# Windowed attention with sinks and a gated MLP block: products of a constant tile put into TensorE's queue before and between the first pairs of heads, and a third load buffer

## The chip, the cores and the metric

The kernel runs on one core of one Trainium2 chip. The metric is the device time of one execution in microseconds (us). A core has five engines with a queue of instructions each, which they work through in order: PE (TensorE, the matrix array; its weight loads are shown apart as PEld), DVE (VectorE), ACT (ScalarE), POOL (GpSimd) and SP (SyncE, which here only issues DMAs).

## What is computed

There are 4 batches, 8 heads, 768 positions and 64 columns per head, all in float32. Attention keeps a window of 128 positions back and the first 4 positions ("sinks"); its output, put together to rows of 512, goes through a gated MLP with a mixing over positions.

```python
def _attn_ref(q, k, v, n_sink, window):          # (4, 8, 768, 64); n_sink 4, window 128
    scores = scale * np.matmul(q, k.transpose(0, 1, 3, 2))
    keep = is_sink | in_window                   # pos < 4, or 0 <= row - pos < 128
    scores = np.where(keep, scores, -1000000000.0)
    ...
    a = a / (np.sum(a, axis=-1, keepdims=True) + 1e-09)
    return np.matmul(a, v)

def _moe_ref(x, w_in, g_ln, w_sg, b_sg, w_out):  # x (4, 768, 512), w_in (512, 1024)
    h = x @ w_in                                 # then gelu (tanh form)
    u, v = (h[..., :d_ff // 2], h[..., d_ff // 2:])
    v_n = (v - mu) / np.sqrt(var + 1e-06) * g_ln
    v_s = np.einsum('ts,bsd->btd', w_sg, v_n) + b_sg[None, :, None]
    return x + (u * v_s) @ w_out
```

## The kernel before, in words

**The unit of work is a pair of heads.** There are 16 pairs, numbered n, four to a batch. A pair has 6 tiles of 128 positions. Its k and q come by two DMAs of 384 KB on SP (`load_qk`, line 80) into float32 buffers `k_sb` and `q_sb` of the pool `loads`, which holds 2 of each. The first pair's come in halves, k on SP and q on ACT's queue (`load_first`, line 95). v comes on POOL's queue, converted to bf16 on the way (`load_v`, line 87), and so do the 4 sink rows of all heads (`vsink`, line 141) and the weights (`load_weights`).

**From load to transposed columns.** `repack` (line 191) has POOL cast k and q to bf16. `keys` and `queries` transpose the six tiles on PE (`to_columns`, line 197: six products with an identity into the PSUM tile `cps`) and ACT copies them out as `kT` and `qT` (line 204). For keys POOL also copies the 4 sink columns to `sk` (line 214). The first pair goes a way of its own, `prepare_first`: for each half of the positions, DVE casts k and q (line 230), PE transposes three tiles of each (line 234), ACT copies k's columns and DVE q's (lines 238 and 240).

**Scores and values.** `score(n, g)` makes four products (line 260) for two of the six tiles and one exponential on ACT (line 264) from PSUM tile `sc`, of which there are two, shared with the sink scores `scs` (line 275, exponential in line 277). `keep_band` multiplies by the band on DVE (line 271). `values(n, i)` multiplies the exponentials with v (lines 305, 308, with the sinks 311) into the PSUM tile `av`, of which there is one; after three tiles DVE takes the reciprocals and scales into `x` (lines 315, 316). `columns` transposes x to `xT` (line 286).

**The order is written out by hand.** Ahead of the loop come the loads of pairs 0 and 1, constants, `prepare_first`, and then `load_qk(2)`, `repack(1)`, `load_v(1)`. In step n of the loop POOL gets `repack(n + 2)`, `load_v(n + 2)` and a part of the weights; PE gets the scores of pair n (groups g = 0, 1, 2), between them the values of pair n - 1, the transposes of keys n + 1 and, in the first batch, of queries n + 1; SP gets `load_qk(n + 3)` after the scores. In step 0 the keys and queries of pair 1 come last, after the sink scores. A load waits until the cast of the pair that had its buffer has read it.

**The MLP** of a batch follows one step after its four pairs: `hidden` makes the products with the input weights (lines 333 and 345, gelu on ACT), and the mixing over positions (line 383) and the output (lines 397 to 409) are queued as fillers among the next batch's scores. A last part of the program, behind a branch, is a slower and safer path that these inputs don't take.

Of the kernel before, what the change touches and what calls it, by code (L numbers as in the profile page):

```python
# [8 lines left out]
F32 = mybir.dt.float32  # L9
BF16 = mybir.dt.bfloat16  # L10
# [7 lines left out]
def kernel(  # L18
# [14 lines left out]
    nc = tc.nc  # L33
# [14 lines left out]
    NH = S // 2  # L48

    consts = ctx.enter_context(tc.tile_pool(name="consts", bufs=1))  # L50
    loads = ctx.enter_context(tc.tile_pool(name="loads", bufs=2))
    work = ctx.enter_context(tc.tile_pool(name="work", bufs=2))
    small = ctx.enter_context(tc.tile_pool(name="small", bufs=4))
    ps_s = ctx.enter_context(tc.tile_pool(name="ps_s", bufs=2, space=PSUM))
    ps_a = ctx.enter_context(tc.tile_pool(name="ps_a", bufs=1, space=PSUM))
# [5 lines left out]
    HT = NT // 2  # L61
# [13 lines left out]
    def load_qk(n):  # L75
        b, hp = divmod(n, HP)
        pair = []
        for src, name in ((k, "k_sb"), (q, "q_sb")):
            dst = loads.tile([128, 2, NT, 64], F32, name=name)
            nc.sync.dma_start(out=dst, in_=src[b, 2 * hp:2 * hp + 2].rearrange(  # L80
                "h (p t) d -> p h t d", t=NT))
            pair.append(dst)
        qk[n] = pair

    def load_v(n):
        b, hp = divmod(n, HP)
        nc.gpsimd.dma_start(  # L87
            out=v_bufs[n % NV][:, :, :, 0:64],
            in_=v[b, 2 * hp:2 * hp + 2].rearrange("h (t p) d -> p h t d", p=128))

    def load_first():
        pair = [loads.tile([128, 2, NT, 64], F32, name=name) for name in ("k_sb", "q_sb")]
        for a in range(2):
            for src, dst, queue in ((k, pair[0], nc.sync), (q, pair[1], nc.scalar)):
                queue.dma_start(
                    out=dst[:, :, HT * a:HT * (a + 1), :],
                    in_=src[0, 0:2, NH * a:NH * (a + 1)].rearrange(
                        "h (p t) d -> p h t d", t=HT))
        qk[0] = pair

    load_first()
    load_qk(1)
    for t in v_bufs[0:2]:
        nc.vector.memset(t[:, :, :, 64:65], 1.0)

# [21 lines left out]
    def copy_masks():  # L127
        nc.vector.tensor_copy(mask0, mask)
        for hl in range(2):
            nc.vector.memset(mask0[0:n_sink, 2 * hl, :], 1.0)  # L130
        for hl in range(2):
            nc.vector.tensor_copy(mask_end[:, 384 * hl:384 * hl + 256], mask[:, 0, :])
            nc.vector.tensor_copy(mask_end[:, 384 * hl + 256:384 * (hl + 1)],
                                  mask[:, 0, 0:128])
# [52 lines left out]
    def repack(n, eng):  # L187
        packed[n] = []
        for src, name in zip(qk.pop(n), ("k_bf", "q_bf")):
            flat = work.tile([128, NT, 128], BF16, name=name)  # L190
            eng.tensor_copy(flat.rearrange("p t (h d) -> p h t d", h=2), src)  # L191
            packed[n].append(flat)

    def to_columns(src, pool, tag):
        ps = pool.tile([128, NT, 128], BF16, name="cps", tag=tag)
        for t in range(NT):
            nc.tensor.transpose(ps[:, t, :], src[:, t, :], iden)  # L197
        return ps

    def copy(eng, dst, src):  # L200
        dst = dst.rearrange("c (p t) -> c p t", t=NT)
        src = src.rearrange("c t p -> c p t")
        if eng is nc.scalar:
            eng.copy(dst, src)  # L204
        else:
            eng.tensor_copy(dst, src)
# [9 lines left out]
    def queries(n, eng, pool, tag):  # L216
        qps = to_columns(packed.pop(n)[1], pool, tag)
        qTs[n] = work.tile([128, S], BF16, name="qT")
        copy(eng, qTs[n], qps)

    def prepare_first():
        flats = [work.tile([128, NT, 128], BF16, name=name) for name in ("k_bf", "q_bf")]
        qTs[0] = work.tile([128, S], BF16, name="qT")
        kT, sk = kT_bufs[0], sk_bufs[0]
        for a in range(2):
            ts = slice(HT * a, HT * (a + 1))
            for src, flat, dst, eng, pool, tag in (
                    (qk[0][0], flats[0], kT, nc.scalar, ps_t, "tp"),
                    (qk[0][1], flats[1], qTs[0], nc.vector, ps_m, "mm")):
                nc.vector.tensor_copy(  # L230
                    flat[:, ts, :].rearrange("p t (h d) -> p h t d", h=2), src[:, :, ts, :])
                ps = pool.tile([128, NT, 128], BF16, name="cps", tag=tag)
                for t in range(HT):
                    nc.tensor.transpose(ps[:, t, :], flat[:, HT * a + t, :], iden)
                to = dst[:, NH * a:NH * (a + 1)].rearrange("c (p t) -> c p t", t=HT)
                frm = ps[:, 0:HT, :].rearrange("c t p -> c p t")
                if eng is nc.scalar:
                    eng.copy(to, frm)
                else:
                    eng.tensor_copy(to, frm)  # L240
            if a == 0:
                for hl in range(2):
                    rows = slice(64 * hl, 64 * hl + 64)
                    nc.gpsimd.tensor_copy(sk[rows, 32 * hl:32 * hl + n_sink],
                                          kT[rows, 0:n_sink])
                score(0, 0)
        qk.pop(0)

    def score(n, g):
        kT, qT = kT_bufs[n % NB], qTs[n]  # L250
        if g == 0:
            exps[n] = work.tile([128, NT * 512 - 256], BF16, name="ex")
        ex = exps[n]
        sc = ps_s.tile([128, 2, 512], F32, name="sc", tag="s")
        w = 0
        for j in (2 * g, 2 * g + 1):
            n_q = min(256, S - 128 * j)
            for hl in range(2):
                rows = slice(64 * hl, 64 * hl + 64)
                nc.tensor.matmul(sc[:, hl, w:w + n_q], kT[rows, 128 * j:128 * (j + 1)],  # L260
                                 qT[rows, 128 * j:128 * j + n_q], start=True, stop=True)
            w += n_q
        part = ex[:, 1024 * g:1024 * g + 2 * w].rearrange("p (h c) -> p h c", h=2)
        nc.scalar.activation(out=part, in_=sc[:, :, 0:w], func=AF.Exp, scale=scale)  # L264

    def keep_band(n, g):
        w = 1024 if g < HT - 1 else 768
        part = exps[n][:, 1024 * g:1024 * g + w]
        m = mask0 if g == 0 else mask
        m = m.rearrange("p a c -> p (a c)") if g < HT - 1 else mask_end  # L270
        nc.vector.tensor_mul(part, part, m)  # L271
# [8 lines left out]
    def by_dma(n):  # L280
        return n >= HP and n % HP < HP - 1
# [135 lines left out]
    def fill(count=1):  # L417
        for _ in range(count):
            if fillers:
                fillers.pop(0)()  # L420
# [142 lines left out]
        V.tensor_copy(mask[:, i, :], mask[:, 0, :])  # L563
    prepare_first()
    copy_masks()
    load_qk(2)
    repack(1, G)
    load_v(1)
    prepare_rest()
# [1 line left out]
    for n in range(NP):  # L571
        if n + 2 < NP:
            repack(n + 2, G)
            load_v(n + 2)
        load_weights(n)
        late = half_valued == n - 1

        def value(i):
            if n > 0 and (i >= HT or not late):
                values(n - 1, i)  # L580

        points = (HT + 1) * ((HP - n) % HP)

        def spread(left):
            if n > HP * (B - 1):
                fill(1 if left > 2 or (left == 1 and n < NP - 1) else 0)
            else:
                fill(-(-len(fillers) // (points + left)))

        for g in range(HT):  # L590
            if n + g > 0:
                score(n, g)
            if g < 2 and not late:
                for i in range(HT * g, HT * (g + 1)):
                    value(i)
            if g == 0 and n > 0 and n + 1 < NP:
                keys(n + 1)
                if n < HP:
                    queries(n + 1, A, ps_m, "mm")
            if g == 0 and late:  # L600
                for i in range(HT, NT):
                    value(i)
            keep_band(n, g)
            if g == 1 and n + 1 < NP and n >= HP:
                queries(n + 1, A, ps_t, "tp")
            spread(HT + 1 - g)
        if n + 3 < NP:
            load_qk(n + 3)
        sinks(n)
        if n == 0:  # L610
            keys(1)
            queries(1, A, ps_m, "mm")
        if n > 0 and not by_dma(n - 1):
            columns(n - 1)
        spread(1)
        if n % HP == 0 and n > 0:
            fill(len(fillers))
            hidden(n // HP - 1, [lambda i=i: values(n, i) for i in range(HT)])
            half_valued = n
# [58 lines left out]
```

## Time and profile before

| | |
|---|---|
| time, median of 3 runs | 180.08 us (179.92 to 180.32) |
| the profiled execution | 180.66 us, of which 178.8 us from the first to the last instruction |
| busy, share of the span | PE 88%, PEld 50%, DVE 82%, ACT 67%, POOL 32% |
| PE products / POOL instructions | 1407 / 98 |
| moved by DMA | 27.24 MB, 152 GB/s on the mean |
| chain that ended last | PE 75%, ACT 12%, issue 4%, DVE 4%, DMA 2% |

All of it is from the page of one profiled execution. A row of slices cuts the span in 40 equal parts of 4.47 us; each digit is the busy share in tenths. A row of the timeline begins with its start and its length in us, then engine, line and operation, the tile written and the tile read, and in brackets how long the engine was idle before it and what ended that. Matmuls overlap and their ends are modelled, so the distance between starts says more than one length. A row of a DMA queue gives packets, MB and the time that its packets took, as a share of the time of 16 engines; q1 is SP's queue, q0 POOL's, q10 ACT's.

### The profile page before, as it was taken

The page shows a single profiled execution, that of the slowest core. Times are in us where ns is not written, and L with a number is a line of the kernel's source. Part 1 is how long each engine was busy: PE and PEld are TensorE (multiplying, and loading weights), DVE is VectorE, ACT ScalarE, POOL GpSimd, SP SyncE. Part 2 cuts the span into 40 slices and gives each one's busy share as a digit, 9 for nine tenths or more (in the row PEclk, how much of TensorE's full clock was granted, in tenths as well). Part 3 has the DMA queues.
Part 4 walks back from the last instruction along what each step waited for, and adds up shares of the span by engine and source line. Part 5 has one row for each costly group of instructions (what it writes and reads, how often), then busy time and mean ns, then how long its engine had stood idle before and what let it go on. Part 6 is the DMA issues. An engine that isn't in the chain of part 4 may idle for free.

```text
span 178.8 us, 3744 instructions
## 1 busy us (share of the span) xinstructions
PE 156.6 (88%) x1407; PEld 88.7 (50%) x1418; DVE 146.0 (82%) x359; ACT 119.4 (67%) x168; POOL 57.5 (32%) x98
## 2 busy tenths in 40 slices
PE   0769779799689999899899999899799999999970
PEld 0447556345556555445456545355465554555430
DVE  5665989599889999698999998699999948858950
ACT  2488999867938668666968668877986856640000
POOL 8459999950042060425006070550010000000000
PEclk9999999999999999999999999999999999999999
DMA  5999999999857739895285969986202241011072
GB/s 158 266 306 265 267 271 273 191 207 218 103 179 48 202 66 209 303 270 39 20 219 33 214 183 192 380 108 44 44 4 44 50 178 59 0 63 60 0 294 66
DMA packets 47974, 27.24 MB, mean 152 GB/s; under 512 B 33680, under 2 KB 44944, under 8 KB 47952
## 3 DMA queue, kind: packets, MB, share of 16 engines
q0 software_dynamic: 27904, 6.31, 37.5%
q1 hardware_dynamic: 19504, 20.26, 37.5%
q10 hardware_dynamic: 544, 0.39, 0.7%
q8 instruction: 12, 0.20, 0.5%
q14 instruction: 10, 0.08, 0.1%
HBM read 24.81 MB, written 6.29 MB: 174 GB/s over the span
## 4 chain that ended last, share of the span: by engine, by line
PE 75%; ACT 12%; issue 4%; DVE 4%; DMA 2%
PE vs L383 17%; PE hu L345 13%; PE o_ps L397 11%; PE hv L333 11%; ACT ex L264 7%; PE sc L260 7%; PE cps L197 5%; PE av L305 4%; ACT kT L204 3%; PE scs L275 2%; PE av L308 2%; DMA k_sb<-in_k_dram 2%; ACT qT L204 2%; PE av L311 1%; DVE ex L271 1%
## 5 line engine op out<-in xcount | busy, mean ns | idle before, releaser
L264 ACT ACTIVATE ex<-sc 128x1024 bf16<-128x1024 f32 (+1 forms) x48 | 45.6, 958 | 16.9 <-PE sc L260 16.7
L383 PE MATMUL vs<-wsgT,vn 128*128 128x384 bf16 x192 | 35.5, 327 | 0.5 <-DVE wsgT L182 0.4
L191 POOL CAST k_bf<-k_sb 128x768 bf16<-128x768 f32 x15 | 12.3, 823 | 42.7 <-DMA k_sb<-in_k_dram 31.8
L397 PE MATMUL o_ps<-w_out_sb,gT 128*128 128x512 bf16 (+1 forms) x93 | 23.8, 370 | 1.2 <-DVE o_sb L401 0.8
L271 DVE TENSOR_TENSOR ex<-ex,mask 128x1024 bf16<-128x1024 bf16 x32 | 23.0, 722 | 1.8 <-ACT ex L264 1.7
L333 PE MATMUL hv<-w_in_sb,xT 128*128 128x512 bf16 x92 | 22.2, 379 | 1.9 <-DVE xT L286 1.7
L383 PEld LDWEIGHTS <-vn 128*128 128x128 bf16 x192 | 17.9, 98 | 12.0 <-issue 1.2
L345 PE MATMUL hu<-xT,w_in_sb 128*128 128x384 bf16 x128 | 23.2, 325 | 0.1
L260 PE MATMUL sc<-qT,kT 64*128 64x256 bf16 x192 | 19.0, 280 | 2.2 <-DVE qT L240 1.3
L386 DVE SCALAR_TENSOR_TENSOR gv<-vs,g_sb,b_bc 128x384 bf16<-128x384 f32 x32 | 19.5, 611 | 1.7 <-PE vs L383 1.7
L348 ACT ACTIVATE uT<-hu 128x384 bf16<-128x384 f32 x32 | 15.7, 490 | 6.5 <-PE hu L345 6.3
L337 DVE BATCH_NORM_STATS2 st<-v_all 128x6 f32<-128x512 f32 x24 | 16.3, 677 | 4.6 <-ACT v_all L335 4.5
L335 ACT ACTIVATE v_all<-hv 128x512 f32<-128x512 f32 x24 | 14.3, 597 | 7.2 <-PE hv L333 6.9
L316 DVE TENSOR_TENSOR x<-av,inverses 128x384 bf16<-128x384 f32 x32 | 17.8, 557 | 1.1
L305 PE MATMUL av<-v_sb,ex 128*128 128x65 bf16 x192 | 18.2, 198 | 0.2 <-DVE x L316 0.2
L305 PEld LDWEIGHTS <-ex 128*128 128x128 bf16 x192 | 14.5, 100 | 7.2 <-issue 2.9
L345 PEld LDWEIGHTS <-w_in_sb 128*128 128x128 bf16 x128 | 12.4, 97 | 10.7 <-issue 2.9
L87 POOL DMA_DIRECT2D v_sb<-in_v_dram x16 | 16.6, 1036 | 0.0
L308 PE MATMUL av<-v_sb,ex 128*128 128x65 bf16 x160 | 16.5, 197 | 0.0
L214 POOL COPY sk<-kT 64x4 bf16<-64x4 bf16 x30 | 6.2, 207 | 28.2 <-ACT kT L204 27.3
L191 POOL CAST q_bf<-q_sb 128x768 bf16<-128x768 f32 x15 | 14.1, 938 | 3.0 <-DMA q_sb<-in_q_dram 2.2
L333 PEld LDWEIGHTS <-xT 128*128 128x128 bf16 x96 | 9.0, 98 | 11.9 <-DVE xT L286 2.6
(83 smaller groups left out, 241.4 us busy)
## 6 DMA issues: line engine op xcount, KB each, us to landing
k_sb<-in_k_dram SPq DMA_DIRECT2D x15, 384.0 KB, 5.5
q_sb<-in_q_dram SPq DMA_DIRECT2D x15, 384.0 KB, 6.1
out_dram<-o_sb SPq DMA_DIRECT2D x17, 256.0 KB, 3.5
v_sb<-in_v_dram POOLq DMA_DIRECT2D x16, 192.0 KB, 6.9
out_dram<-o_act SPq DMA_DIRECT2D x6, 256.0 KB, 2.0
wsg_sb<-in_moe_w_sg_dram POOLq DMA_DIRECT2D x2, 576.0 KB, 10.2
w_in_sb<-in_moe_w_in_dram POOLq DMA_DIRECT2D x4, 256.0 KB, 8.9
w_out_sb<-in_moe_w_out_dram POOLq DMA_DIRECT2D x1, 512.0 KB, 11.8
```

The costliest lines, as they stand in the source:

```text
L191: eng.tensor_copy(flat.rearrange("p t (h d) -> p h t d", h=2), src)
L260: nc.tensor.matmul(sc[:, hl, w:w + n_q], kT[rows, 128 * j:128 * (j + 1)], qT[rows, 128 * j:128 * j + n_q], start=True, stop=True)
L264: nc.scalar.activation(out=part, in_=sc[:, :, 0:w], func=AF.Exp, scale=scale)
L271: nc.vector.tensor_mul(part, part, m)
L305: nc.tensor.matmul(av[:, m, hl, :], probs(i, hl, 0), v_sb[:, hl, i, :], start=(m == 0 and hl == 0), stop=False)
L308: nc.tensor.matmul(av[:, m, hl, :], probs(i - 1, hl, 1), v_sb[:, hl, i - 1, :], start=False, stop=False)
L316: nc.vector.tensor_mul(x_sb[b][:, hp, HT * c:HT * (c + 1), :].rearrange("p i (h d) -> p i h d", h=2), av[:, :, :, 0:64], rcp.to_broadcast( ...
L333: nc.tensor.matmul(h_ps, xT[b][:, c, 128 * j:128 * (j + 1)], w_in_sb[:, c, DF:], start=(c == 0), stop=(c == KD - 1))
L345: nc.tensor.matmul(h_ps[:, 0:NH], w_in_sb[:, c, 128 * f:128 * (f + 1)], xT[b][:, c, NH * n:NH * (n + 1)], start=(c == 0), stop=(c == KD - 1))
L383: nc.tensor.matmul(vs[:, 0:NH], vns[b][:, si, 128 * f:128 * (f + 1)], wsgT[:, si, cols], start=(si == 0), stop=(si == NT - 1))
L386: nc.vector.scalar_tensor_tensor(out=gv, in0=vs[:, 0:NH], scalar=g_sb[:, f:f + 1], in1=b_bc[:, cols], op0=ALU.mult, op1=ALU.add)
L397: nc.tensor.matmul(o_ps, gTs[b][:, c, rows], w_out_sb[:, c, cols], start=(c == 0), stop=(c == KU - 1 and whole))
```

## The change

The pool `loads` gets 3 buffers of each tile, and `load_qk(2)` moves from behind `prepare_first` to right behind `load_qk(1)`. DVE sets a tile of 128 x 128 to ones, and a function `keep_busy(count)` has PE multiply this tile with itself that many times, into a PSUM tile that takes the place of `av` and is never read. It is called with 28 ahead of all other work on PE, with 7 at the end of each of the two halves of `prepare_first` (behind its transposes and copies, ahead of the first scores), with 6 after the last scores of step 0, and with 8 after the queries of pair 1.

```diff
-    loads = ctx.enter_context(tc.tile_pool(name="loads", bufs=2))
+    loads = ctx.enter_context(tc.tile_pool(name="loads", bufs=3))
...
     load_first()
     load_qk(1)
+    load_qk(2)
+    warm = consts.tile([128, 128], BF16, name="warm")
+    nc.vector.memset(warm, 1.0)
+    warm_ps = ps_a.tile([128, HT, 2, 65], F32, name="warm_ps", tag="av")
+
+    def keep_busy(count):
+        for _ in range(count):
+            nc.tensor.matmul(warm_ps[:, 0].rearrange("p h d -> p (h d)")[:, 0:128],
+                             warm, warm, start=True, stop=True)
+
+    keep_busy(28)
     for t in v_bufs[0:2]:
...
                     eng.tensor_copy(to, frm)
+            keep_busy(7)
             if a == 0:
...
     copy_masks()
-    load_qk(2)
     repack(1, G)
...
             if n + g > 0:
                 score(n, g)
+            if n == 0 and g == HT - 1:
+                keep_busy(6)
...
             queries(1, A, ps_m, "mm")
+            keep_busy(8)
```

## The prediction

> **What bounds the kernel now.** I read the page's slices first, then the products by shape before and after 18 us, then the order of time up to 30 us, the windows and the DMA queues.
>
> ```profile
> PE   0769779799689999899899999899799999999970
> ACT  2488999867938668666968668877986856640000
> PEclk9999999999999999999999999999999999999999
> ```
>
> Each slice is 4.47 us. From about 38 us the PE row is full, and the chain of waits is nearly all PE; a gain made earlier is kept if nothing else is late. The clock row shows nothing of a slow start, but the durations do. The groups by shape, first for 0 to 18 us, then for 19 to 33 us (the column after the bar is the mean of one in ns):
>
> ```profile
> L260 PE MATMUL sc<-qT,kT 64*128 64x256 bf16 x20 | 3.0, 400 | 2.2 <-DVE qT L240 1.3 <-ACT qT L204 0.9
> L197 PE MATMUL cps<-iden,k_bf 128*128 128x128 bf16 x12 | 1.7, 313 | 0.0
> L275 PE MATMUL scs<-qT,sk 128*128 128x512 bf16 x2 | 1.2, 596 | 0.8 <-ACT ex L264 0.8
> ...
> L260 PE MATMUL sc<-qT,kT 64*128 64x256 bf16 x26 | 2.8, 274 | 0.0
> L197 PE MATMUL cps<-iden,k_bf 128*128 128x128 bf16 x18 | 1.5, 219 | 0.0
> L275 PE MATMUL scs<-qT,sk 128*128 128x512 bf16 x3 | 1.1, 376 | 2.2 <-ACT ex L264 2.1
> ```
>
> The same shapes are 220 ns faster for 512 columns and 94 ns for 128, so the array runs at half rate at first. The timeline fixes the moment: six transposes from 17.66 still take 0.68, four score products at 18.27 take 0.39 (0.61 before). Twelve transposes in a row from 13.76 are 0.107 apart, those from 18.97 0.056. The windows say what came before: PE was busy 4.55 of 7.50 us in 5.00 to 12.50 without a switch, then 5.61 of 5.70 in 12.50 to 18.20, with the switch at the end.
>
> ACT then is the limit of pairs 2 to 4: 14.13 busy of 14.30 us in 18.20 to 32.50. Timeline rows, start and length:
>
> ```profile
> 4.38 0.50 PE L234 MATMUL cps<-iden,k_bf 128*128 128x128 bf16 x3 [4.38 <-DVE k_bf L230]
> 4.89 0.50 PE L234 MATMUL cps<-iden,q_bf 128*128 128x128 bf16 x3
> 5.43 0.56 DVE L240 COPY qT<-cps 128x384 bf16<-128x384 bf16 x1 [0.59 <-PE cps L234]
> 7.45 0.56 DVE L240 COPY qT<-cps 128x384 bf16<-128x384 bf16 x1 [0.92 <-PE cps L234]
> ...
> 6.69 1.02 ACT L264 ACTIVATE ex<-sc 128x1024 bf16<-128x1024 f32 x1 [1.30 <-PE sc L260]
> 8.70 1.73 ACT L264 ACTIVATE ex<-sc 128x1024 bf16<-128x1024 f32 x2 [0.61 <-PE sc L260]
> 13.23 1.02 ACT L264 ACTIVATE ex<-sc 128x1024 bf16<-128x1024 f32 x1 [0.70 <-PE sc L260]
> 14.72 0.80 ACT L204 COPY kT<-cps 128x768 bf16<-128x768 bf16 x1 [0.47 <-PE cps L197]
> 18.71 1.02 ACT L264 ACTIVATE ex<-sc 128x1024 bf16<-128x1024 f32 x1
> 19.63 0.79 ACT L204 COPY kT<-cps 128x768 bf16<-128x768 bf16 x1
> 23.24 1.02 ACT L264 ACTIVATE ex<-sc 128x1024 bf16<-128x1024 f32 x1
> ```
>
> Before 18 us ACT idles behind PE (the brackets); after it, it doesn't. So what the change can win is how much earlier ACT reaches the first exponential of pair 2, at 18.71.
>
> **The change part by part.**
>
> *28 products first.* They need a memset (0.07, before DVE's first one at 1.01), so PE starts near 1.15 and at 0.107 each ends near 4.15. The first transposes wait for a cast until 4.38: they cost nothing, with 0.2 us of cover. They make PE's work nearly unbroken from 1.15 on. How long that takes to double the rate the trace bounds by at most 5.6 us (12.6 to 18.2): the switch then falls between 4.4, from which on it matters, and 6.8. I take 6.8, the one length that the trace shows to be enough.
>
> The Trainium skill's page "TensorE: Matmul & The Clock Gate" (Part 4: PE-mode transpose) says against this that transposes don't count as busy in the same way. By it the stretch with 12 transposes after 4.38 might not count, and the switch would come only after 12 us: the sum below would be -0.95 less the DMA term. The trace bears it out only in part, since the stretch before 18.2 holds 24 transposes and did switch.
>
> *Seven after each half of the first pair.* They stand behind q's transposes and ahead of the scores, which wait for DVE's copy. At half rate: 4.89 + (3 + 7) x 0.107 = 5.96, and the scores began at 6.04; in the second half 6.88 + 1.07 = 7.95 against 8.06. The cover is 0.1 us even at half rate: nothing. The six (0.34 at full rate) lie under the exponential that the sinks product waits for, the eight (0.45) under ACT's copies of pair 1.
>
> *What full rate from 6.8 changes.* Up to 6.65 nothing moves. The second scores (8.06) wait for ACT's copy of k's second half, 7.61 + 0.47, as before; they take 0.39, not 0.61, so ACT starts their exponential at 8.47 (was 8.70). ACT is then closed: 1.70 to the sinks exponential, 0.64 to the keys and 0.69 to the queries of pair 1, whose copy starts at 11.50 (was 11.73). The scores of pair 1 come 0.86 after that, at 12.36, and take 0.42 with the handover, not 0.64: exponential at 12.78, **-0.45**. From it to ACT's copy of the next keys took 1.49 (13.23 to 14.72), behind values and transposes at half rate; the same step is 0.92 one pair later (18.71 to 19.63): **-0.57**. From there to the next pair's exponential took 3.99 (14.72 to 18.71), and takes 3.61 where ACT is closed (19.63 to 23.24): **-0.38**. Together -1.40: pair 2's exponential at 17.31. With full rate from 4.4 on the first scores too end earlier (6.26, not 6.65), which adds 0.37.
>
> *Third pair's loads early.* They go out on SP directly behind the second pair's, at about 2.8 and 3.3 instead of 6.28 and 6.76, and every later pair finds a buffer one pair sooner. What it gives: POOL's cast of pair 2 waits less. What it costs: 768 KB stand ahead of v's loads.
>
> ```profile
> 11.94 0.82 POOL L191 CAST k_bf<-k_sb 128x768 bf16<-128x768 f32 x1 [1.91 <-DMA k_sb<-in_k_dram]
> ...
> q1 hardware_dynamic: 158, 0.24, 85.5%
> ...
> q1 hardware_dynamic: 753, 1.09, 105.2%
> ```
>
> The cast can begin at 10.0. ACT wants these keys at 13.7, and even before they were cast by 12.76 and the queries by 13.8: worth 0 to 0.1. The two queue rows are of 8 to 10 and of 10 to 13 us: full speed is 363 GB/s, thus 2.2 us for a pair, and 8 to 10 us moved only 0.29 MB in all (0.05 on POOL's queue), so 1.3 us of that was unused and is filled now. The need for v, moved up with the chain: v of pair 0 (requested at 2.28, 8.2 to landing) goes from 10.5 to at most 12.7, wanted at 12.6 (first value product, 13.13 before). The last sink rows (11.3) go to 13.5, wanted at 12.9: 0.6 late, ahead of pair 2's transposes on PE, whose copy would then start at 14.1, not 13.7. v of pair 1 (8.96 + 7.5 = 16.5) goes by 2.2 - 1.3 to 17.4, wanted at 17.2 (18.59 before), 17.6 if the sink rows were late. Pair 3's has 0.2 to spare. The last quarter of the input weights (27.04 + 9.3 = 36.3, used at 38.01) has no more bytes ahead of it than before, and POOL asks for it earlier: nothing. So between 0 (requests on POOL's queue not held up) and 0.6; the landings are worked out at their latest, so I take **+0.3**.
>
> *Later.* SP waits once less per load; POOL's long waits for loads after 50 us are a pair ahead of need. PE, ACT and DVE do the same work after pair 0: nothing.
>
> Sum: -0.45 - 0.57 - 0.38 + 0.30 = -1.1. The profiled execution took 180.66 with 178.8 of span (1.86 outside it); it would take 179.56. The 0.58 that it lies above the median is not touched, so from the median of 180.08: **179.0**.
>
> **The rivals.**
>
> *Slower: v starved.* If the DMA engines served SP's queue until it is empty, v of pair 0 would wait for pairs 2, 3 and 4: SP's requests of 6.28 and 7.58, which were for pairs 2 and 3, are now for 3 and 4 and keep the queue full to 7.1 + 3 x 2.2 = 13.7, not 7.1. v lands 6.6 - 1.3 = 5.3 later, at 15.8. Values of pair 0 stand on PE ahead of pair 2's transposes and start 2.7 late; the 0.95 after it stays: +1.7, or 181.8. It decides from a landing later than 14.1. For it: from 10 to 13 us POOL's queue moved nothing, although v of pair 1 had been issued by 10.02. Against it: order of arrival explains that too, and from 17 to 18 us POOL's queue had 182.1% and SP's 25.7% with a load of SP's requested at 16.84.
>
> The skill's page "DMA: Bandwidth & Descriptors" (Queues, rings and completion order) states a round robin between queues. By it v would share from its issue on, land before its need, and the +0.3 would fall away: -1.4. The row of 10 to 13 us speaks against it.
>
> *Same: no earlier switch,* since a product of ones doesn't count or the gaps at 4.2 and 4.8 reset it. The products are covered at half rate too, so nothing moves but loads: 180.1.
>
> *Same or little: given back.* v's landings 1.3 worse (the unused time from 8 to 10 us isn't there to fill): v of pair 1 at 18.7, 0.1 later than used before; what is left is 0 to 0.4: 179.9.
>
> *More: earlier switch and no late v.* -1.40 - 0.37: 178.3.
>
> **How the numbers follow.** Forecast (-0.4 to -1.5): 0.56. Earlier switch: 0.12. No switch 0.05 and given back 0.10. Starved: 0.17. A measurement of this kernel tells 0.2%, 0.36 us, from no change. Faster 0.68, same 0.15, slower 0.17. The range leaves out only the starved case: from 178.2 (the earlier switch, less 0.1 of spread between runs) to 180.3 (given back, plus the 0.2 to 0.4 by which the runs spread).
>
> **What would show it.** Score products of about 280 ns from 8 us on instead of 400; pair 1's first exponential near 12.8 and pair 2's near 17.6; ACT closed from 13 to 31; the first hidden product near 31.8 (was 32.94); POOL's cast of pair 2 near 10. I am wrong if the rate is half past 9 us, if values of pairs 0 or 1 wait for a DMA by over 0.6 us, or if the first hidden product moves by 1 and the end doesn't.

## The result, and the profile after

Before: 180.2 us (179.92 to 180.67, 4 executions); after: **186.14 us** (184.76 to 187.50, 4). The ratio is 1.0303 [1.0255, 1.035]: the change makes the kernel slower by 3%, where 179.0 was forecast and the range ended at 180.3. The profiled execution took 186.01, of which 184.2 of span, 5.4 more than before. A ratio given here leaves out the few executions that ran clearly longer than the rest of the same kernel; medians are over all.

The slices of the page (4.6 us each):

```profile
PE   7842967879969999989979999899799999999970
ACT  2661889987793776767796687967987667650000
PEclk9997599999999999999999999999999999999998
```

The PE row begins with a 7 instead of a 0: the products of ones. But the fourth slice (14 to 18 us) is a 2 on PE and a 1 on ACT, and the clock row, flat before, now dips there and in the slice behind it. From 38 us the rows look as before. The chain of waits says what stands in the hole: first its shares by engine, then two of its longest pieces, with start and length.

```profile
PE 56%; DMA 15%; DVE 13%; ACT 8%; issue 4%; SPq 1%; POOL 0%; ACTq 0%
```

```profile
2.33 5.67 DMA q_sb<-in_q_dram
8.82 14.85 DMA v_sb<-in_v_dram
```

DMA had 2% of the chain before and has 15%. A load of v (of pair 1) that POOL asked for at 8.82 landed at 23.67; before, the same load was asked for at 8.96 and took 7.5. The timeline of PE and ACT (start, length, in brackets the idle time and its cause):

```profile
1.21 3.17 PE L110 MATMUL warm_ps<-warm 128*128 128x128 bf16 x28 [1.21 <-DVE v_sb L115]
6.06 0.39 PE L272 MATMUL sc<-qT,kT 64*128 64x256 bf16 x4
13.34 1.02 ACT L276 ACTIVATE ex<-sc 128x1024 bf16<-128x1024 f32 x1 [0.48 <-PE sc L272]
15.95 0.33 PE L317 MATMUL av<-v_sb,ex 128*128 128x65 bf16 x3 [2.64 <-DMA v_sb<-in_v_dram]
18.02 0.29 PE L323 MATMUL av<-vsink,exs 128*128 128x130 bf16 x1 [1.36 <-DMA vsink<-in_v_dram]
19.06 0.80 ACT L215 COPY kT<-cps 128x768 bf16<-128x768 bf16 x1 [4.70 <-PE cps L208]
23.16 1.02 ACT L276 ACTIVATE ex<-sc 128x1024 bf16<-128x1024 f32 x1 [0.17 <-PE sc L272]
23.71 0.25 PE L317 MATMUL av<-v_sb,ex 128*128 128x65 bf16 x3 [0.60 <-DMA v_sb<-in_v_dram]
38.46 0.39 PE L345 MATMUL hv<-w_in_sb,xT 128*128 128x512 bf16 x1 [1.26 <-DVE xT L298]
```

The second row is the change's success: four score products take 0.39 at 6.06, which they took only from 18.27 on before. Then PE stands 2.64 us for v of pair 0 and 1.36 for the sink rows. Pair 2's transposes are queued behind these products, so ACT copies the keys of pair 2 at 19.06, not 14.72 (+4.34), and begins pair 2's exponentials at 23.16, not 18.71 (+4.45). v of pair 1 costs 0.60 more, a wait of PE for DVE at 34.58 another 0.38 (0.62 against 0.24), and the first hidden product starts 5.52 late (38.46 against 32.94). The span is 5.4 longer, so everything is lost by then.

Why v is late is in the queue rows, first of the changed kernel from 15 to 18 us, with the load that POOL issues there (192 KB, 14.1 us to landing), then from 20 to 22 us, then of the kernel before from 7 to 8 us (packets, MB, share of 16 engines' time):

```profile
q1 hardware_dynamic: 589, 0.86, 91.1%
q0 software_dynamic: 591, 0.07, 35.8%
...
v_sb<-in_v_dram POOLq DMA_DIRECT2D x1, 192.0 KB, 14.1
...
q1 hardware_dynamic: 386, 0.57, 90.9%
q0 software_dynamic: 387, 0.05, 37.4%
```

```profile
q0 software_dynamic: 1108, 0.14, 217.8%
q1 hardware_dynamic: 27, 0.03, 10.6%
```

In these two stretches of the changed kernel the packets of the two queues pass **one for one**. But a packet of SP's is 0.86 MB / 589 = 1.5 KB, and one of POOL's about 0.12 KB. v of a pair is 192 KB in 1536 packets of 128 B: at 591 in 3 us they need 7.8 us, at the 1108 per us that POOL's queue had while SP's was empty, 1.4. With three buffers SP's queue has work with few gaps up to 22 us (requests for four more pairs between 2.8 and 12.4), so v seldom has the fast turn. This counts from the first packet of a load on; that comes late in both kernels (v of pair 0, requested at 2.3, moves none before 6 us).

### The profile page after: what moved, and what is told of

Its sections match the earlier page's. It is cut to its first block, busy times and chain, and to the rows that moved or that the text cites. A ratio compares the mean times of both kernels' runs of the same rounds, so it can differ in the third digit from the quotient of the medians.

```text
span 184.2 us, 3861 instructions
## 1 busy us (share of the span) xinstructions
PE 159.8 (87%) x1463; PEld 92.4 (50%) x1474; DVE 147.4 (80%) x360; ACT 119.6 (65%) x168; POOL 57.3 (31%) x98
## 4 chain that ended last, share of the span: by engine, by line
PE 56%; DMA 15%; DVE 13%; ACT 8%; issue 4%; SPq 1%; POOL 0%; ACTq 0%
PE vs L395 16%; PE o_ps L409 10%; DMA v_sb<-in_v_dram 8%; PE hv L345 6%; PE hu L357 6%; PE sc L272 5%; ACT ex L276 4%; PE cps L208 4%; DMA out_dram<-o_sb 4%; PE av L317 3%; DMA q_sb<-in_q_dram 3%; DVE st L349 3%; DVE ex L283 2%; ACT kT L215 2%; PE av L320 2%
## 5 line engine op out<-in xcount | busy, mean ns | idle before, releaser
L283 DVE TENSOR_TENSOR ex<-ex,mask 128x1024 bf16<-128x1024 bf16 x32 | 24.6, 773 | 2.2 <-ACT ex L276 2.2
L202 POOL CAST k_bf<-k_sb 128x768 bf16<-128x768 f32 x15 | 12.7, 844 | 40.1 <-DMA k_sb<-in_k_dram 18.9
L317 PE MATMUL av<-v_sb,ex 128*128 128x65 bf16 x192 | 18.2, 198 | 4.0 <-DMA v_sb<-in_v_dram 3.2
L272 PE MATMUL sc<-qT,kT 64*128 64x256 bf16 x192 | 18.4, 270 | 2.5 <-ACT qT L215 2.1
L225 POOL COPY sk<-kT 64x4 bf16<-64x4 bf16 x30 | 6.7, 224 | 37.4 <-ACT kT L215 36.6
L357 PEld LDWEIGHTS <-w_in_sb 128*128 128x128 bf16 x128 | 12.4, 97 | 10.7 <-issue 2.9
L215 ACT COPY kT<-cps 128x768 bf16<-128x768 bf16 x15 | 11.9, 792 | 5.2 <-PE cps L208 5.2
```

What stands on the lines that cost most here:

```text
L317: nc.tensor.matmul(av[:, m, hl, :], probs(i, hl, 0), v_sb[:, hl, i, :], start=(m == 0 and hl == 0), stop=False)
L357: nc.tensor.matmul(h_ps[:, 0:NH], w_in_sb[:, c, 128 * f:128 * (f + 1)], xT[b][:, c, NH * n:NH * (n + 1)], start=(c == 0), stop=(c == KD - 1))
```

## The experiments

The first six ask which part costs and by what mechanism, the others why the part that worked brings nothing.

**e1: products alone** (against the changed kernel).

```diff
-    loads = ctx.enter_context(tc.tile_pool(name="loads", bufs=3))
+    loads = ctx.enter_context(tc.tile_pool(name="loads", bufs=2))
...
-    load_qk(2)                  # behind load_qk(1)
...
+    load_qk(2)                  # behind copy_masks(), as before
```

> The four groups of products with two load buffers, the loads requested as before. Theory A (all of the loss comes from v's loads, held up on POOL's queue by one pair more on SP's): v of pair 0 lands near 10.5 us as before, the full rate comes at about 5.5 us, and the steps of the prediction without its DMA term hold: pair 2's first exponential near 17.3 instead of 18.71, time 1.0 to 1.4 below before, about 178.8. Theory B (the products themselves harm, by their place in PE's queue or by what an earlier rate does to the rest): above 180.5.

180.86 us; ratio 0.9994 [0.9962, 1.0026] against the kernel before: no change. ACT's rows of the timeline, PE's first row after the start of the hidden products (32.41), and the chain's piece before it:

```profile
12.54 1.02 ACT L275 ACTIVATE ex<-sc 128x1024 bf16<-128x1024 f32 x1 [0.48 <-PE sc L271]
13.53 0.80 ACT L214 COPY kT<-cps 128x768 bf16<-128x768 bf16 x1
17.42 1.02 ACT L275 ACTIVATE ex<-sc 128x1024 bf16<-128x1024 f32 x1
...
18.09 0.25 PE L316 MATMUL av<-v_sb,ex 128*128 128x65 bf16 x3 [0.71 <-DMA v_sb<-in_v_dram]
...
33.39 0.24 PE L316 MATMUL av<-v_sb,ex 128*128 128x65 bf16 x2 [0.59 <-DMA v_sb<-in_v_dram]
```

```profile
22.18 11.16 DMA v_sb<-in_v_dram
```

The products do what they were forecast to do: pair 2's exponential is 1.29 earlier than before (18.71). Then v of pair 1 is 0.71 late, and v of pair 4, asked for at 22.18 (21.76 before), lands at 33.34 instead of 31.9. The lead of 1.29 is 0.53 at the first hidden product (32.94 before) and gone behind the wait of 0.59. A third loss comes later: from 49.78 to 53.20 us the granted clock of this execution is 0.50, where the kernel before has 1.00 all the way. The first twelve mixing products, in the kernel before and then in e1, show the price:

```profile
50.97 2.11 PE L383 MATMUL vs<-wsgT,vn 128*128 128x384 bf16 x12 [0.40 <-DVE wsgT L182]
```

```profile
51.21 3.09 PE L394 MATMUL vs<-wsgT,vn 128*128 128x384 bf16 x12
```

They begin 0.24 late and end 1.22 late. In how many of the other executions this happens was not recorded.

**e2: loads alone** (against the changed kernel): all products of ones taken out.

```diff
-    keep_busy(28)
...
-            keep_busy(7)
...
-            if n == 0 and g == HT - 1:
-                keep_busy(6)
...
-            keep_busy(8)
```

> Three load buffers and the early request, none of the products. Theory A: v of pair 0 lands at 15 to 16 us, its sink rows near 18, v of pair 1 near 23.7, and the end moves with the last of these: 185 to 187, no better than the whole change. Theory B: the loads alone cost little, 180 to 181. If the half rate after the 2.6 us wait carries a part of the loss of its own, this kernel, which is at half rate until about 20 us anyway, comes out between the two or above the whole change.

186.36 us; ratio 1.0314 [1.028, 1.0348], the whole loss. PE's timeline:

```profile
17.00 0.32 PE L306 MATMUL av<-v_sb,ex 128*128 128x65 bf16 x3 [3.98 <-DMA v_sb<-in_v_dram]
19.44 0.29 PE L312 MATMUL av<-vsink,exs 128*128 128x130 bf16 x1 [1.73 <-DMA vsink<-in_v_dram]
```

**e3: the rate held.** The wait from 13.3 to 16 lets the rate fall back to half (granted clock 0.50 from 15.8 to 22.6). Is that part of the cost? Against the changed kernel:

```diff
+            if n == 1 and g == 0:
+                keep_busy(50)
```

> The whole change with 50 more products (about 2.8 us at full rate) between the scores of pair 1 and the first values, so that PE does not idle while v of pair 0 is awaited. Theory A1 (the chain is that of v of pair 1, landing at 23.7 us): the rate stays full past 16 us, but the end stays within 0.5 us of the whole change, near 186. Theory A2 (the half rate from 15.8 to 22.6 us is what costs): 1.3 to 2 us below the whole change, near 184.3.

187.23 us; ratio 1.0357 [1.0311, 1.0403]. The rate stays full to 19.28, 3.5 us longer; v still comes at 16.56 and the sink rows at 18.82, and the keys are copied at 19.50. The time is no better, 1.1 above the changed kernel where at most 0.5 was expected. With e2, whose products are at half rate until about 23 us and which loses the same, this says that the loads are the cost and not the lower rate.

**e4: the first 28 alone**, without the loads' change. Against the changed kernel, with 2 buffers and the request at its old place as in e1:

```diff
-            keep_busy(7)
...
-            if n == 0 and g == HT - 1:
-                keep_busy(6)
...
-            keep_busy(8)
```

> Two load buffers and only the 28 products ahead of the first loads, none between the first pairs. If the 28 fill what the switch needs, the full rate comes near 5.5 us and stays, and the time is that of all products with two buffers, 178.8 within 0.2. If the gaps between the first half copies break it, the rate comes later, or falls back between 8 and 18 us, and the time lies between 179.2 and 180.2.

181.25 us; ratio 1.002 [0.9987, 1.0053]. The rate is full from 5.04 to 8.45, then half until 18.7, and pair 2's exponential is at 19.05 (17.42 in e1). Over all executions the mean granted clock is 0.951 to 0.971 in nine of twelve, and in e1 it is 0.988 or more in eleven of twelve. So the small fills, which cost nothing, keep the early rate; the time shows no difference between the two kernels.

**e5: which half of the loads' change?** Against the changed kernel, 3 buffers kept:

```diff
-    load_qk(2)                  # behind load_qk(1)
...
+    load_qk(2)                  # behind copy_masks(), as before
```

> All products and three load buffers, with the request for the third pair left at its old place in the program. SP has nothing between the two places and waits only for a free buffer, so if the third buffer is what matters, nothing changes against the whole change: 185 to 187.5, the request goes out at about 2.8 us, and v of pair 0 lands after 15 us. If the place matters, the request goes out at about 6.3 us and the time is near 181.

187.25 us; ratio 1.0366 [1.0317, 1.0414]. The request goes out at 2.84 as in the changed kernel, since SP has nothing else to wait for. The place in the program is nothing, the buffer is all.

**e6: small packets on SP's queue too.** If the queues take turns packet by packet, k and q in packets of 256 B must let v through; if SP's queue is served until it is empty, nothing changes. Against the changed kernel:

```diff
+            form = "h (p t) d -> p h t d" if n < 2 else "h (t p) d -> p h t d"
...
-                "h (p t) d -> p h t d", t=NT))
+                form, t=NT))
```

> The whole change, but k and q of pairs 2 to 15 are loaded with 64-column rows of 256 bytes in place of runs of 1536 (their positions are then permuted, so this leaves the attention of these pairs undone as the reference has it; only the landings count). Theory R (each DMA engine takes one packet of SP's queue and one of POOL's in turn, whatever their size): v of pair 0 now meets packets six times smaller, gets near half of the time and lands at 10 to 13 us instead of 15.8; the pairs' own loads land later. Theory Q (the engines serve SP's queue until it is empty, or in the order of arrival): v lands at 15 us or later, since the same bytes stand ahead of it in more packets.

186.88 us in one execution. The queue rows from 7.5 to 9.5 us, and PE's two waits:

```profile
q1 hardware_dynamic: 921, 0.28, 84.6%
q0 software_dynamic: 709, 0.09, 68.8%
```

```profile
13.07 0.25 PE L318 MATMUL av<-v_sb,ex 128*128 128x65 bf16 x3 [0.35 <-DMA v_sb<-in_v_dram]
14.02 0.23 PE L324 MATMUL av<-vsink,exs 128*128 128x130 bf16 x1 [0.48 <-DMA vsink<-in_v_dram]
```

v of pair 0 lands 10.7 after its request instead of 13.5, and the waits of 2.64 and 1.36 shrink to 0.35 and 0.48 with the same buffers and bytes. So the size of SP's packets decides when v lands. That speaks for turns by packet and against a queue that is served until it is empty, though the counts here are not one for one and it is a single execution. The time doesn't follow, since k and q in small packets come late themselves: PE waits 0.53 and 1.21 for POOL's casts of pair 2, and loads of k and q hold 16% of the chain.

**e7 and e8: v first.** If e1 fails for late v, POOL could ask for v (and the weights) before it casts. Without products (e7, against the kernel before) and with them and 2 buffers (e8):

```diff
-            repack(n + 2, G)
             load_v(n + 2)
...
+        if n + 2 < NP:
+            repack(n + 2, G)
```

> The kernel before, without products and with two load buffers, but in each step POOL issues v's load and the weights ahead of the casts of k and q, not behind them. POOL's 1.9 us of idle ahead of the cast of pair 2 then holds 1.75 us of issues, and v of pair 4 is asked for 1.6 to 3 us earlier than at 21.76. Theory: ACT is still the limit of pairs 2 to 4 and v of pair 4 was not late before, so this alone gives 0 to 0.3: 180.0 to 180.7 with 180.67 beside it. If it gains over 0.6, POOL's chain was a limit of the kernel before by itself.

> The same order on POOL with all four groups of products and two load buffers. Theory P (with products alone the gain of 1.3 us at pair 2's exponential was given back by v of pairs 1 and 4, waited for at 18.1 and 33.4 us): with v asked for earlier both waits go, the first hidden product comes near 31.6 and the time is 1.0 to 1.4 below the kernel before run beside it. Rival: POOL's or the DMA engines' own work is full in this stretch, v of pair 4 lands near 33 as before, and the time stays within 0.4 of the kernel before.

e7: 181.27 us; 1.0051 [1.0023, 1.0078]. e8: 180.65 us; 1.0013 [0.9995, 1.0031]. The order alone makes the kernel a little slower (e7, where 0 to 0.3 us of gain was expected), so beside e7 the products of e8 are worth 0.6 us in the medians. e8 has no wait for v left, and pair 2's exponential at 17.41, but the first hidden product at 32.97. The lead is lost in between, on DVE and POOL (e8's timeline, then POOL's):

```profile
21.14 1.29 DVE L282 TENSOR_TENSOR ex<-ex,mask 128x1024 bf16<-128x1024 bf16 x1
22.36 1.17 DVE L282 TENSOR_TENSOR ex<-ex,mask_end 128x768 bf16<-128x768 bf16 x1
```

```profile
21.07 0.82 POOL L201 CAST k_bf<-k_sb 128x768 bf16<-128x768 f32 x1
21.83 1.29 POOL L201 CAST q_bf<-q_sb 128x768 bf16<-128x768 f32 x1
```

Two such mask products take 0.69 and 0.56 in the kernel before at 22.09 and 22.79. Where a mask product and a cast fall beside each other, both take longer; that happens in the kernel before too (a mask product of 1.25 at 19.88, a cast of 1.29 at 20.53). In e8 it falls on the chain: from 16 to 34 us DVE's mask products are the largest piece of it, with 26.1%.

**e9 and e10: lighter casts.** v first, and from pair 2 on the casts cut to a sixth, without (e9) and with (e10) the products; both against the kernel before, e10 with the `keep_busy` calls added.

```diff
+    flat_bufs = [[consts.tile([128, NT, 128], BF16, name=f"{name}{i}") for i in range(2)]
+                 for name in ("k_bf", "q_bf")]
...
-        for src, name in zip(qk.pop(n), ("k_bf", "q_bf")):
-            flat = work.tile([128, NT, 128], BF16, name=name)
-            eng.tensor_copy(flat.rearrange("p t (h d) -> p h t d", h=2), src)
+        ts = slice(0, NT) if n < 2 else slice(0, 1)
+        for src, bufs in zip(qk.pop(n), flat_bufs):
+            flat = bufs[n % 2]
+            eng.tensor_copy(flat[:, ts, :].rearrange("p t (h d) -> p h t d", h=2),
+                            src[:, :, ts, :])
```

> The control for the next kernel: no products, two load buffers, v's load first on POOL, and POOL's casts of k and q cut to one of six tiles from pair 2 on (the other tiles keep older pairs' values, so the attention of these pairs isn't done; POOL has some 1.3 us less per pair and collides less with DVE). ACT is still the limit of pairs 2 to 4 and PE is at half rate until about 18 us: within 0.5 of the kernel before, pair 2's exponential near 18.7.

> The same with all four groups of products. Theory C (with v asked for early, what took the products' 1.3 us was POOL's casts running beside DVE's mask products, which took 1.1 to 1.3 us each instead of 0.55 to 0.70): with the casts mostly gone pair 2's exponential comes near 17.4, the first hidden product near 31.6, and the time is 1.0 to 1.4 below the control. Rival: something else in pairs 2 to 4 (the DMA engines, ACT's order) takes it; then pair 2's exponential is early, the first hidden product is not, and the time is within 0.4 of the control.

e9: 180.13 us; 0.9988 [0.9957, 1.0019]. e10: 180.11 us (178.37 to 182.86); ratio 0.9939 [0.9907, 0.997]. With POOL mostly out of the way the products are worth 0.5% by the ratios, but the two intervals overlap and the medians are 0.02 us apart: at most a small gain, and not the 1.0 to 1.4 us of theory C. e10's profiled execution took 181.63, above its median; it is read for the order of events only:

```profile
31.25 0.39 PE L351 MATMUL hv<-w_in_sb,xT 128*128 128x512 bf16 x1 [1.11 <-DVE xT L304]
32.97 0.29 PE L323 MATMUL av<-v_sb,ex 128*128 128x65 bf16 x2 [1.33 <-DMA v_sb<-in_v_dram]
```

The first hidden product keeps 1.7 us of lead, and then v of pair 4 takes 1.33 of it: asked for at 16.55, it landed 16.4 later. PE is busy 1.09 of the 3.41 us ahead of 32.80, the granted clock is 0.50 from there to 36.21, and the lead turns into a delay (hidden products of line 363 begin at 39.22, those of the kernel before at 37.84). With the casts light, SP's buffers come free early, and the queues share one for one again (from 17 to 21 us 590 packets of SP's, 582 of POOL's).

**e11: only pair 2's loads early.** Pair 0 gets buffers of its own, so that no later load comes earlier. Against the changed kernel, with 2 buffers and `load_qk(2)` at its old place:

```diff
-        pair = [loads.tile([128, 2, NT, 64], F32, name=name) for name in ("k_sb", "q_sb")]
+        pair = [consts.tile([128, 2, NT, 64], F32, name=name) for name in ("k_first", "q_first")]
```

> All products; the first pair has buffers of its own, so the third pair's loads go out at 2.8 us as in the whole change, but the later pairs wait for their casts as in the kernel before. One pair instead of three stands beside v of pair 0. By one packet of each queue in turn (1536 packets of v, 512 of a pair of k and q, some 184 per us of each while both wait) v still meets pair 2 and, from 8.8 us on, pair 3: it lands at 13 to 14.5 instead of 15.8, the sink rows up to 15.5, and the time is 182 to 185. If one pair is harmless, v lands before 12.7 and the time is at or below that of the products alone.

181.16 us; ratio 1.0028 [0.9993, 1.0063]. PE's timeline:

```profile
13.10 0.25 PE L316 MATMUL av<-v_sb,ex 128*128 128x65 bf16 x3 [0.69 <-DMA v_sb<-in_v_dram]
```

One pair early puts v of pair 0 at 13.0 and costs 0.69, no more: less than I expected of the time. The loss in the changed kernel comes from the queue that stays full behind it.

**e12, e13, e14: SP held back.** A small copy of v of pair 4 on SP, ahead of the load of pair 6, makes SP wait until v has landed. With light casts and v first (e12), in the whole computation as in e1 (e13), and with v first (e14):

```diff
+    landed = consts.tile([1, 64], BF16, name="landed")
...
+        if n == 3:
+            nc.sync.dma_start(out=landed, in_=v_bufs[4 % NV][0:1, 0, 0, 0:64])
```

> The light casts with products (POOL's casts cut to one of six tiles from pair 2 on, attention of these pairs not done), and before the load of pair 6 SP gets a small copy out of v's buffer of pair 4, so that pairs 6 and 7 are asked for only when that has landed. Theory D (what was left of the wait was v of pair 4 again sharing packet for packet with k and q of pairs 6 and 7): v of pair 4, asked for at 16.6 and landed 16.4 later, lands by 28, the wait of 1.3 us at the first hidden products goes, and the time is 1.2 to 1.6 below the light control's 180.1, near 178.7. Rival: its landing is set by the bytes of POOL's own queue ahead of it; it stays near 33 and the time stays near 180.

> A whole kernel: products with two load buffers and the same hold of pairs 6 and 7. With products alone the first hidden product came at 32.4 (32.94 before) and v of pair 4 was waited for until 33.4. Theory D: that wait goes, the wait of 0.7 for v of pair 1 at 18.1 stays, and the time is 0.4 to 0.8 below the kernel before. Rival: pairs 6 and 7 come too late for POOL's casts, or v isn't earlier: no gain.

> A whole kernel: as the last, with v's load first on POOL. Neither wait for v is left, but POOL's casts run beside DVE's mask products as in the order with v first, where the first hidden product came at 33.0 without any wait for v: within 0.4 of the kernel before if that collision is what holds it, 1.0 or more below if it isn't.

e12: 179.77 us; 0.9935 [0.9906, 0.9964], no better than e10. v of pair 4 now lands at 29.5 and nothing waits for it, but the wait has moved to v of pair 2, asked for at 10.68 (chain, then PE):

```profile
10.68 12.57 DMA v_sb<-in_v_dram
```

```profile
23.30 0.25 PE L324 MATMUL av<-v_sb,ex 128*128 128x65 bf16 x3 [1.40 <-DMA v_sb<-in_v_dram]
```

e13: 184.14 us; 1.0163 [1.0118, 1.0208], slower. With SP held, v of pair 4 lands 7.7 after its request, not 11.2 as in e1, which points to the loads of k and q beside it there. The first hidden product is at 33.30, with no wait for v ahead of it, but the held loads hold POOL's casts, and behind these the request for the mixing weights:

```profile
48.96 1.10 PE L191 MATMUL wps<-iden,wsg_sb 128*128 128x128 bf16 x9 [2.54 <-DMA wsg_sb<-in_moe_w_sg_dram]
```

e14: 181.77 us; 1.0032 [0.9998, 1.0065]: no wait for v, the first hidden product at 32.63, DVE 22% of the chain, and the granted clock at 0.50 from 49.54 to 52.96, as in e1. That it ends 0.9 us above the kernel before in the medians, and not within 0.4, was not expected. No version with the whole computation beat the kernel before; e1 and e8 equal it.

## Why the prediction was wrong

**The 28 products: right.** They end by 4.4 and the first transposes start at 4.45 (4.38 before). The rate is full by 6.06 (four score products in 0.39), earlier than the 6.8 that I took. The Trainium skill's rule by which transposes don't count as busy ("TensorE: Matmul & The Clock Gate", Part 4: PE-mode transpose) would have put the switch after 12 us; no such delay is seen here, though 28 products ahead of the transposes leave the rule itself untested.

**The sevens, the six and the eight: right**, and needed to keep the early rate (e4).

**-0.45, -0.57, -0.38: right where the loads are left as they were.** In e1 the three marks are at 12.54, 13.53 and 17.42, forecast 12.78, 13.70 and 17.31: -1.29 for -1.40. That the sum is so close is partly luck: the single steps are -0.69, -0.50 and -0.10. The first is larger because the first scores already ran at the full rate; the last is a quarter of what I took from the pair after it. In the changed kernel the first mark is at 13.34, since ACT's sink exponential waited 0.90 for DVE there. POOL's cast of pair 2, forecast near 10, is at 9.88, and did harm instead of good: beside it two of DVE's mask products took 1.47 and 1.32 (0.66 and 0.67 in e1, with the cast at 12.03).

**"Third pair's loads early", +0.3: the step that failed.** Alone it measured +5.7 (e2, 186.36 against 180.67 for the kernel before), by far the largest term. I worked it out in bytes (768 KB at 363 GB/s ahead of v) and in order of arrival, with the unused 1.3 us to soften it: v of pair 0 at most at 12.7, the sink rows at 13.5, v of pair 1 at 17.4. They came at 15.8, 18.0 and 23.7, and PE's wait of 2.64 for v of pair 0 is the sign of being wrong that the prediction had named (over 0.6). The queues were served neither in order of arrival nor by bytes: they passed a packet each in turn (589 to 591, 386 to 387), and v is made of packets a twelfth the size. "Every later pair finds a buffer one pair sooner" stands in the text as a gain; it is what kept SP's queue full.

**The rival "v starved": right in sign, right in its landing (15.8) by luck, wrong in mechanism and too cheap.** It had SP's queue served until empty; the rows from 15 to 18 us, where both queues move, and e6 speak against that. It priced v of pair 0 alone at +1.7. The sink rows, on the same queue behind v, added 1.36 on PE, and v of pair 1 0.60 more.

**The evidence I weighed it down with was misread.** "From 17 to 18 us POOL's queue had 182.1%" was a second in which SP's queue passed hardly anything (69 packets against 911). From 18 to 19 us it passed nothing at all, although its load had been requested at 16.84: no packet of that load had begun (the next one is at 19.4), so the row was no evidence on sharing. "10 to 13 us: POOL's queue moved nothing" was likewise a load that had not started yet; what holds up such a start I can't say. The sentence on the Trainium skill's round robin ("DMA: Bandwidth & Descriptors", Queues, rings and completion order) drew from it that v would land before its need; the page speaks of turns by packet, and the trace agrees: 589 packets to 591. By that rule v's 1536 packets beside a full queue cost 7.8 us, not 1.4: 6.4 more, where v of pair 0 measured 13.5 - 8.2 = 5.3 and v of pair 1 14.8 - 7.5 = 7.3. That several descriptors pass in one turn, as the page also says, no run here shows.

**"Later: nothing": wrong too, and hidden by the larger miss.** v of pair 4 was not in my list of needs. It landed at 31.9 before, and I had the hidden products move up to 31.8 with its use 0.5 behind. e1 shows it 0.59 late, and e8, e10 and e12 that when one such wait is taken away, another engine or load takes its place: from 18.2 to 32.5 us before, not only ACT was full (14.13 of 14.30 us) but POOL (13.93) and nearly DVE (12.50). So even without the extra buffer the forecast of -1.1 would have failed: "given back" was its outcome, through v of pairs 1 and 4 rather than pair 1 alone. In e1's profiled execution, whose span is 1.2 longer than the kernel before's, the times of the marks divide the loss: some 0.7 us at v of pair 1, 0.8 around v of pair 4, and 1.0 in the half rate from 49.78 on. For that last one I had no term ("PE, ACT and DVE do the same work after pair 0: nothing"). e8, whose rate stays full until PE's last products, loses its lead on DVE and POOL instead. That POOL's casts alone take it is not shown; e10 gives at most 0.5% back.

## What to carry to other kernels

Before a load gets another buffer, count the packets, not the bytes, that each queue will have waiting: a queue of small packets beside one that was always full moved one small packet per large one here. List every load in the stretch against its new time of need, those of the stage behind it too. A faster rate of PE bought early is kept only while PE stays busy, so look for its later gaps as well. And where several engines are nearly full in a stretch, a lead won on one of them is mostly given back within a few steps.

## What the runs showed of the hardware that was not expected

- Two DMA queues with work waiting passed 589 and 591 packets in 3 us, at 1.5 KB and 0.12 KB each, and 386 and 387 in 2 us; with 256-B packets on the first queue, 921 and 709 in 2 us.
- PE's rate fell back to half 2.5 us after it went idle (13.3 to 15.8), and in e4 at 8.45 with several short gaps ahead and no long one. In all 16 profiles the time from one change of the granted clock to the next is a whole multiple of 3.41 us, apart from the last stretch of each. PE was busy 0.39 us of the 3.41 ahead of the fall at 15.78, 1.69 ahead of that at 8.45 and 1.87 ahead of e1's at 49.78. The kernel before has the same gaps between 45 and 51 us; counted from its own switch they lie in two such stretches, busy 2.09 and 2.62, and its rate holds. So it may be chance, set by when the switch came, that e1 fell back there and the kernel before did not. A sharp threshold these runs don't show: the changed kernel held its rate over a stretch with 1.49 (8.96 to 12.37).
- A mask product on DVE (0.69 us) and a cast on POOL (0.82) took 1.29 each when they ran beside each other.
